# Decode attention beside a gated FFN: engine instructions in written order, and the masked weights one slot later

## The chip, the cores and the metric

The kernel runs on one core of a Trainium2 chip. The metric is the device time in microseconds (us) of one execution. Engines: PE is the matmul engine, DVE the vector engine, ACT the scalar engine; SP only issues the loads and the final store. In the traces here every engine runs its instructions in the order in which they were compiled for it (DVE's 471, for instance, before and after), and this case is about what that order is. In the tables, "span" is the length of the profiled execution, about 1.8 us shorter than its device time.

## The reference

```python
# B=4 sequences, 1 new token, D=640; H=32 heads, Dh=192, 8192 keys, of which the last W=2048 count
xn = layernorm(x)
q = (xn @ wq) -> [4, 32, 1, 192]
scores = einsum("bhqd,bhkd->bhqk", q, k_cache[:, :, -W:]) * 192**-0.5
o = einsum("bhqk,bhkd->bhqd", softmax(scores), v_cache[:, :, -W:])
attn = o.reshape(4, 1, 32 * 192) @ wo
ffn = (silu(xn @ w1) * (xn @ w3)) @ w2        # F = 1536
return x + attn + ffn                          # all bf16
```

The work is dominated by bytes: 32 heads, each with a K tile and a V tile of 3 MiB.

## The kernel before

A head's K lies in SBUF as 128 rows (32 key groups of 4 sequences) of 64 keys. A head is worked in four quarters `u` of 16 keys. DVE multiplies K by q (`mult`), PE adds up each key's six groups of 32 products with an identity matrix (`adder`, 6 matmuls), DVE reduces the 32 sums that are left (`reduce_quarter`). Then comes the maximum over all keys (`chain_*`), the exponential on ACT, the masked weights `z` (DVE), and 32 value matmuls (`pv`, 8 per quarter). At the end of each pair of heads there is the pair's end (`ge_*`): totals `tb`, reciprocals `rtb`, transposes `gp` of the value sums `o_raw`, normalised `oT`, and the projection with the pair's part of `wo`.

```python
kpool = ... bufs=KBUFS   # 2 K tiles        vpool = ... bufs=VBUFS   # 3 V tiles
wopool = ctx.enter_context(tc.tile_pool(name="wo", bufs=2))
...                                          # all loads are issued on nc.sync, one queue
def mult(u):                                 # DVE
    pr = ppool.tile([P, JQ, Dh], BF16, tag="pr")
    mi = nc.vector.tensor_tensor(out=pr[:], in0=kts[h][...], in1=qbc[...], op=ALU.mult)
def adder(u):                                # PE: 6 identity matmuls 128x512
def reduce_quarter(u):                       # DVE; asked to stay behind mult(u + 2)
    ri = nc.vector.tensor_reduce(out=scs[h][...], in_=pss.pop(u)[:], axis=AX.X, op=ALU.add)
    tc.add_manual_dep(ri.ins, mult_insts[ahead].ins.name, ORDER_DEP, ...)
def chain_bc(h):                             # PE, ACT, DVE
    ...
    nc.scalar.activation(out=ex[:], in_=scs.pop(h)[:], func=ACTF.Exp, ...)
    nc.vector.tensor_tensor(out=z[:], in0=ex[...], in1=mask_b[...], op=ALU.mult)
def pv(u):                                   # PE: 8 value matmuls 8x384
...
for h in range(H):                           # the slots; u0, ul = first, last quarter of h
    if h >= KBUFS:
        add((h - KBUFS + 1) * GQ, 0, load_k, h)
    add((h - VBUFS) * GQ + GQ + L, 0, load_v, h, ...)          # L = 10
    for u in range(u0, ul + 1):
        add(u, 1, mult, u); add(u + 1, 2, adder, u)            # slot, phase within it
        add(u + 2, 4, reduce_quarter, u); add(u + L, 3, pv, u)
    add(ul + 2, 5, chain_lmax, h); add(ul + 3, 4, chain_tr, h)
    add(ul + 4, 5, chain_gmax, h); add(ul + 5, 4, chain_bc, h)
for hg in range(NG):                         # a pair of heads
    a = (hg + 1) * HG * GQ - 1 + L
    add(a - GQ - L if hg < NG - 1 else a - L + 3, 0, wo_load, hg)
    add(a - 2, 6, ge_sum, hg); add(a - 1, 6, ge_tot, hg); add(a, 6, ge_norm, hg)
    add(a + 1, 3, ge_tr, hg); add(a + 2, 2, ge_copy, hg); add(a + 3, 3, ge_proj, hg)
... # FFN pieces (cut)
for s in sorted(sched): ...                  # the functions are called slot by slot, phase by phase
```

Before, a scheduler reorders what is written. The compiled order on PE and DVE is therefore not the slots' order. Listed from the compiled programs, with `x` counts of matmuls, a pair of heads runs like this:

```
PE : sums x12, max transpose, sums x12, max broadcast, values x32,
     sums x12, max transpose, sums x12, max broadcast, values x24, tb, values x8, gp, projection
DVE: ... gmax, gneg, z, mult, reduce, mult, reduce, mult, lmax, reduce, mult, reduce,
     gmax, gneg, z, rsm, rtb, oT, mult, reduce, ...
```

## Time and profile before

The time before was 594.14 us, the median of 3 executions (593.74 to 596.72).

| before | us |
|---|---|
| span of the profiled execution | 595.0 |
| first multiply / first multiply of the last head | 31.6 / 558.3 |
| a pair of heads in the second half | 34.14 |
| what DMA would need for a pair: 13.07 MB at 427 GB/s | 30.6 |
| drain: from the last head's first multiply to the end | 36.7 |

The pair is an average over the heads 15 to 31: the time between their first multiplies, divided by 8.

The page of the kernel before: first the busy time of each engine, then, in 40 equal slices, the granted TensorE clock in tenths, the busy share of the DMA engines in tenths, and what they moved.

```profile
PE 493.5 (83%) x2339; PEld 239.4 (40%) x2339; DVE 345.6 (58%) x471; ACT 50.4 (8%) x151; POOL 1.1 (0%) x8
...
PEclk9898979799797979989797988979798997979798
DMA  8999999999999998989799898979899798979900
GB/s 362 430 429 425 421 435 422 438 387 427 427 427 392 407 439 333 431 322 428 320 430 396 359 431 329 429 316 431 348 403 431 324 427 334 427 321 417 357 1 0
```

The slices two to eight lie between 421 and 438 GB/s. From the sixteenth slice (about 223 us) on, most second slices fall to 316 to 333: DMA is made to wait. The Trainium skill, "HBM Reference", Specifications (TRN2), gives about 425 GB/s for a core that streams alone, and the trace agrees. No engine is full. The waits view of the kernel before says who stood still and for what (engine, line, what it was about to make, whom it waited for: us in all, times, longest):

```profile
DVE oT L292 <- PE gp L282: 65.2, 16, 8.2
DVE z L240 <- ACT ex L237: 65.1, 31, 3.4
DVE rtb L274 <- PE tb L269: 59.9, 15, 4.4
PE o_ps L251 <- DVE z L240: 36.7, 30, 2.5
PE ps L196 <- DVE sc L204: 29.4, 49, 1.2
...
DVE pr L184 <- DMA kt<-in_A_k_cache_dram: 0.6, 1, 0.6
```

The multiplies hardly ever wait for K.

K is freed by the fourth multiply of a head. The load queue's own waits (SPq; line 91 loads K) and its timeline show it:

```profile
SPq L91 <- DVE pr L184: 426.5, 29, 21.1
```

```profile
409.16 0.53 SPq L91 DMA_DIRECT2D kt<-in_A_k_cache_dram  x1
430.55 0.54 SPq L91 DMA_DIRECT2D kt<-in_A_k_cache_dram  x1
443.30 0.53 SPq L91 DMA_DIRECT2D kt<-in_A_k_cache_dram  x1
```

The queue stands 426.5 us for multiplies, and K loads are issued alternately 21.4 and 12.75 us apart. In 21.4 us DMA could move 9.1 MB at 427 GB/s (an estimate), but the K and V issued at its start are 6.3 MB.

### The profile page before, as it was taken

What the parts mean: (1) busy time and instruction counts of PE and PEld (TensorE: products, weight loads), DVE (VectorE), ACT (ScalarE), POOL (GpSimd) and SP (SyncE); (2) the same over time, 40 slices, a digit from 0 to 9 for tenths busy, and PEclk for the clock granted to TensorE, in tenths of its full rate; (3) what the DMA queues carried; (4) which work ended last, traced back from release to release, by engine and by line L of the source; (5) the groups of instructions that cost most, each with busy time, mean ns of one, the idle gap of its engine ahead of it and who ended that gap; (6) DMA issues with size and microseconds to landing.
All of it is one profiled execution on the core that took longest, in us unless ns stands there. A gap on an engine that the chain in (4) does not pass through costs nothing.

```text
span 595.0 us, 5593 instructions
## 1 busy us (share of the span) xinstructions
PE 493.5 (83%) x2339; PEld 239.4 (40%) x2339; DVE 345.6 (58%) x471; ACT 50.4 (8%) x151; POOL 1.1 (0%) x8
## 2 busy tenths in 40 slices
PE   2857878889988888888888888878888888888887
PEld 1323434444544344434344343434444343433444
DVE  2197376676437748284765838285664828467531
ACT  2101100003210100001000000000010000001010
POOL 0000000000000000000000000000000000000000
PEclk9898979799797979989797988979798997979798
DMA  8999999999999998989799898979899798979900
GB/s 362 430 429 425 421 435 422 438 387 427 427 427 392 407 439 333 431 322 428 320 430 396 359 431 329 429 316 431 348 403 431 324 427 334 427 321 417 357 1 0
DMA packets 13000, 223.31 MB, mean 375 GB/s; under 512 B 1448, under 2 KB 1456, under 8 KB 4144
## 3 DMA queue, kind: packets, MB, share of 16 engines
q1 hardware_dynamic: 12976, 222.97, 89.0%
q8 instruction: 18, 0.29, 0.2%
q14 instruction: 6, 0.05, 0.0%
HBM read 222.96 MB, written 0.01 MB: 375 GB/s over the span
## 4 chain that ended last, share of the span: by engine, by line
PE 55%; DVE 36%; ACT 5%; DMA 3%; issue 1%; SPq 0%; ACTq 0%
PE o_ps L251 30%; DVE pr L184 22%; PE ps L196 12%; DVE sc L204 10%; PE gp L282 6%; DMA wt<-in_A_wq_dram 3%; ACT ex L237 2%; DVE z L240 2%; PE qps L168 2%; PE mt L230 2%; ACT o_raw L259 1%; PE gt L319 1%; DVE oT L292 1%; ACT negm L233 1%; PE tb L269 1%
## 5 line engine op out<-in xcount | busy, mean ns | idle before, releaser
L196 PE MATMUL ps<-pr,idb 128*128 128x512 bf16 x768 | 210.3, 426 | 32.3 <-DVE sc L204 29.4
L184 DVE TENSOR_TENSOR pr<-kt,qbc 128x3072 bf16<-128x3072 bf16 x128 | 223.9, 1750 | 1.0 <-DMA kt<-in_A_k_cache_dram 0.6
L251 PE MATMUL o_ps<-vt,z 128*8 128x384 bf16 x1024 | 178.1, 331 | 37.0 <-DVE z L240 36.7
L196 PEld LDWEIGHTS <-idb 128*128 128x128 bf16 x768 | 80.5, 107 | 154.2 <-issue 91.7
L251 PEld LDWEIGHTS <-z 128*8 128x8 bf16 x1024 | 86.2, 88 | 113.1 <-DVE z L240 39.3
L204 DVE TENSOR_REDUCE sc<-ps 128x16 f32<-128x512 f32 x128 | 87.7, 685 | 15.5 <-PE ps L196 15.3
L240 DVE TENSOR_TENSOR z<-ex,mask_b 128x256 bf16<-128x256 bf16 x32 | 13.6, 425 | 65.1 <-ACT ex L237 65.1
L292 DVE TENSOR_TENSOR oT<-gp,rtb 64x12 bf16<-64x12 f32 x32 | 5.4, 168 | 65.4 <-PE gp L282 65.2
L282 PE MATMUL gp<-idf,o_raw 8*128 8x4 f32 x192 | 36.1, 313 | 8.4 <-ACT o_raw L259 8.4
L282 PEld LDWEIGHTS gp<-idf,o_raw 8*128 8x128 f32 x192 | 34.7, 257 | 14.4 <-ACT o_raw L259 14.3
L274 DVE RECIPROCAL rtb<-tb 128x8 f32<-128x8 f32 x16 | 3.3, 208 | 60.1 <-PE tb L269 59.9
L259 ACT COPY o_raw<-o_ps 8x384 f32<-8x384 f32 x32 | 15.0, 468 | 191.5 <-PE o_ps L251 191.5
L233 ACT COPY negm<-mt 128x1 f32<-128x1 f32 x32 | 5.1, 159 | 306.9 <-PE mt L230 306.9
L301 PE MATMUL acc_231<-wo_t,oT 128*4 128x512 bf16 x48 | 25.6, 601 | 6.6 <-DVE oT L292 6.2
L168 PE MATMUL qps<-wt,xnT 128*128 128x512 bf16 x60 | 17.2, 456 | 5.6 <-DMA wt<-in_A_wq_dram 5.6
L174 DVE CAST qbc<-qps 128x512 bf16<-128x512 f32 x6 | 3.8, 685 | 19.5 <-PE qps L168 19.5
L302 PE MATMUL acc_232<-wo_t,oT 128*4 128x128 bf16 x48 | 14.8, 309 | 0.0
L230 PEld LDWEIGHTS mt<-ones_ff,gneg 1*128 1x128 f32 x64 | 9.4, 182 | 13.5 <-issue 13.5
L168 PEld LDWEIGHTS <-xnT 128*128 128x128 bf16 x60 | 6.8, 113 | 15.6 <-issue 10.5
L230 PE MATMUL mt<-ones_ff,gneg 1*128 1x1 f32 x64 | 12.1, 256 | 0.0
L301 PEld LDWEIGHTS <-oT 128*4 128x4 bf16 x48 | 5.3, 110 | 16.9 <-issue 8.3
L237 ACT ACTIVATE ex<-sc,negm 128x64 bf16<-128x64 f32 x32 | 11.1, 348 | 1.0
(60 smaller groups left out, 104.8 us busy)
## 6 DMA issues: line engine op xcount, KB each, us to landing
kt<-in_A_k_cache_dram SPq DMA_DIRECT2D x32, 3072.0 KB, 13.5
vt<-in_A_v_cache_dram SPq DMA_DIRECT2D x31, 3072.0 KB, 20.9
wo_t<-in_A_wo_dram SPq DMA_DIRECT2D x16, 480.0 KB, 18.7
wt<-in_A_wq_dram SPq DMA_DIRECT2D x2, 3072.0 KB, 13.3
vt<-in_A_v_cache_dram SPq DMA_DIRECT2D x4, 768.0 KB, 14.0
w_718<-in_B_w_dram SPq DMA_DIRECT2D x1, 1920.0 KB, 15.2
w_930<-in_B_w_dram SPq DMA_DIRECT2D x1, 1920.0 KB, 16.8
wt<-in_A_wq_dram SPq DMA_DIRECT2D x1, 1536.0 KB
```

The lines of the kernel that those rows point to most:

```text
L168: nc.tensor.matmul(qp[:], lhsT=xnT[:, kc].rearrange("p a b -> p (a b)"), rhs=wq_rows[kc][:, (c0 + i) * QC:(c0 + i + 1) * QC], start=(kc == ...
L184: mi = nc.vector.tensor_tensor(out=pr[:], in0=kts[h][:, g * JQ:(g + 1) * JQ, :], in1=qbc[:, h * Dh:(h + 1) * Dh].unsqueeze(1).to_broadcast ...
L196: nc.tensor.matmul(ps[:], lhsT=idb[:], rhs=pr[:, :, kk * DD:(kk + 1) * DD], start=(kk == 0), stop=(kk == NK - 1))
L204: ri = nc.vector.tensor_reduce(out=scs[h][:, g * JQ:(g + 1) * JQ], in_=pss.pop(u)[:], axis=AX.X, op=ALU.add)
L230: nc.tensor.matmul(mt[:, P:P + 1], lhsT=gneg[:].rearrange("o p b -> o (p b)"), rhs=ones_ff[0:1, 0:1], start=True, stop=True)
L237: nc.scalar.activation(out=ex[:], in_=scs.pop(h)[:], func=ACTF.Exp, bias=negm[:, 0:1], scale=SCALE, accum_out=rsums[hg][:, hl:hl + 1])
L240: nc.vector.tensor_tensor(out=z[:], in0=ex[:].unsqueeze(2).to_broadcast([P, NJ, B]), in1=mask_b[:].unsqueeze(1).to_broadcast([P, NJ, B]), ...
L251: nc.tensor.matmul(o_ps[:], lhsT=z[:, j:j + 2, :], rhs=vt[:, j:j + 2, :], start=(j == 0), stop=(j == NJ - 2))
L259: nc.scalar.copy(out=o_raws[hg][:, :, hl, :], in_=o_pss.pop(h)[:].rearrange("r (two d) -> r two d", two=2))
L282: nc.tensor.matmul(gp[:, i, :], lhsT=orf[:, part * QW + i:(part + 1) * QW:RPP], rhs=idf[0:2 * B, part * B:(part + 1) * B], start=(part == ...
L301: nc.tensor.matmul(acc0[:], lhsT=oT[:, i, :], rhs=wo_t[:, i * D:i * D + N0], start=st, stop=sp)
L302: nc.tensor.matmul(acc1[:], lhsT=oT[:, i, :], rhs=wo_t[:, i * D + N0:(i + 1) * D], start=st, stop=sp)
```

## The change

Its intent: no scheduler, so that every engine takes its instructions in the order in which the slots are written. `z` gets a function and a slot of its own, one slot after the exponential, so that DVE need not stand behind ACT.

```diff
+    ctx.enter_context(tc.manual_schedule())
 ... (mult_insts, ORDER_DEP and the add_manual_dep in reduce_quarter are removed)
     def chain_bc(h):
         ...
         nc.scalar.activation(out=ex[:], in_=scs.pop(h)[:], func=ACTF.Exp, ...)
+        exs[h] = ex
+
+    def chain_z(h):
+        ex = exs.pop(h)
         z = small.tile([P, NJ, B], BF16, tag="z")
         nc.vector.tensor_tensor(out=z[:], in0=ex[...], in1=mask_b[...], op=ALU.mult)
 ...
         add(ul + 5, 4, chain_bc, h)
+        add(ul + 6, 5, chain_z, h)
```

Afterwards, PE alternates 6 sums and 8 values of a head that is nine quarters older. On DVE, two multiplies with their reductions lie between gneg and z. The pieces of the pair's end lie one slot apart from each other. The order of the loads does not change.

More of the change, by code (lines that the diff above doesn't have):

```diff
@@ L83 @@
     v_win = A_v_cache[:, :, Sk - W:Sk, :]
-    kts, vts, prs, pss, scs, zs = {}, {}, {}, {}, {}, {}
+    kts, vts, prs, pss, scs, exs, zs = {}, {}, {}, {}, {}, {}, {}
     wos, o_pss, o_raws, rsums, chs, ges = {}, {}, {}, {}, {}, {}
-    mult_insts = {}
-    ORDER_DEP = mybir.DependencyInfo(mybir.DependencyClass.NoSync, mybir.DependencyReason.SCHED_ONLY)
     def load_k(h):
@@ L183, in mult @@
         pr = ppool.tile([P, JQ, Dh], BF16, tag="pr")
-        mi = nc.vector.tensor_tensor(out=pr[:], in0=kts[h][:, g * JQ:(g + 1) * JQ, :],
-                                     in1=qbc[:, h * Dh:(h + 1) * Dh].unsqueeze(1).to_broadcast([P, JQ, Dh]),
-                                     op=ALU.mult)
+        nc.vector.tensor_tensor(out=pr[:], in0=kts[h][:, g * JQ:(g + 1) * JQ, :],
+                                in1=qbc[:, h * Dh:(h + 1) * Dh].unsqueeze(1).to_broadcast([P, JQ, Dh]),
+                                op=ALU.mult)
         prs[u] = pr
-        mult_insts[u] = mi
         if g == GQ - 1:
@@ L203, in reduce_quarter @@
             scs[h] = small.tile([P, NJ], FP32, tag="sc", name="sc")
-        ri = nc.vector.tensor_reduce(out=scs[h][:, g * JQ:(g + 1) * JQ], in_=pss.pop(u)[:], axis=AX.X, op=ALU.add)
-        ahead = min(u + 2, NU - 1)
-        if ahead in mult_insts and ahead > u:
-            tc.add_manual_dep(ri.ins, mult_insts[ahead].ins.name, ORDER_DEP, reason="vector engine issue order")
+        nc.vector.tensor_reduce(out=scs[h][:, g * JQ:(g + 1) * JQ], in_=pss.pop(u)[:], axis=AX.X, op=ALU.add)
     def chain_lmax(h):
```

## The prediction

> **What bounds the kernel now.** A serial hand-over between PE and DVE, not one engine. In the steady state (timeline, 400 to 434 us) two heads take 34.15 us. Their traffic, two K tiles, two V tiles and one output-weight tile, is 13.07 MB. Where the DMA share is 1.00 (windows 60:100 and 140:180) the core moves 427 GB/s, which makes 30.6 us. The Trainium skill, "HBM Reference", Specifications, gives about 425 GB/s for a core streaming alone; the trace agrees. From 220 us on, the DMA share falls to 0.84 to 0.94: K loads are issued 21.4 and 12.75 us apart, because a K buffer frees only when the head's fourth multiply is done. PE is idle 101.5 of 595 us; the waits view gives 36.7 us for the masked weights z (about 1.2 per head), 29.4 for score reductions, 8.4 for o_raw, 6.2 for oT. DVE is busy only 58%. Multiplies hardly wait for K (0.6 us in all): DMA follows compute.
>
> **What the change does.** No arithmetic, bytes or buffers change. Before, the scheduler puts all 32 value matmuls of a head in one block straight after z, and two quarters of score sums together; at each pair's end value block, transposes, oT and next multiply run in series. After, PE alternates 6 score sums with 8 value matmuls of work nine quarters older, and z, gmax, oT each stand a slot or more ahead of their users. So the exposed latencies should go.
>
> **Cost per pair after.** PE: eight slots of 1.46 us (6 sums) + 1.46 us (8 value matmuls) = 23.4; transposes 2.25; projection 1.6 to 2.8; max chains and totals about 2: some 29.5 us at full clock, less where groups overlap. DVE: eight times 2.27 plus about 3 = 21. Both are under DMA's 30.6 us. So I expect the bound to become DMA: K landing.
>
> The clock: after each transpose phase PE ran sums every 0.43 instead of 0.22 us for about 5 us. The Trainium skill, "TensorE: Matmul & The Clock Gate", Part 1, gives half clock after an idle window of about 3.4 us; the trace fits (0.56 wait, 2.25 of tiny matmuls, 0.44 wait). With other matmuls around them these cold stretches should become rarer, granted clock from 0.905 to about 0.95; but PE now waits for K in gaps, which may keep some.
>
> **Sum.** Bytes: 223.3 MB at 427 GB/s = 523, plus 2.5 of start: last load lands near 525 (before: near 565). The last K lands some 20 us earlier; from there I count about 47 us: four slots 12, remaining value work, transposes and projections 25, final FFN matmuls (now behind the last projection) 4 to 5, output 5. The tail after the last load stays about 28 us (before 29.5). 525 + 28 = 553; a little for imperfect queueing: 555 us. Range 543 to 573. Faster by over 2%: 0.93, within: 0.06, slower: 0.01.
>
> **What would show it.** DMA share 0.97 or more and about 425 GB/s up to 520 us; multiplies waiting for K tens of us; PE's waits for z and sc near zero; PE busy still near 480 to 500; value groups of 8.
>
> **What would make it wrong.** PE cold more often, so that a pair costs PE 32 us or more (then about 575); output-weight loads, which wait in the one load queue for a projection, holding up the next K; value buffers freeing later and stalling V loads; a longer drain, since ten quarters of value work are left at the end.

## More of the kernel before

The timeline of the kernel before, around the end of a pair (start, duration, instruction; in brackets the idle time of its engine before it, and who ended it):

```profile
412.25 0.42 DVE L240 TENSOR_TENSOR z<-ex,mask_b 128x256 bf16<-128x256 bf16 x1 [2.08 <-ACT ex L237]
412.59 0.16 DVE L263 TENSOR_TENSOR rsm<-rsum,mask_f 128x8 f32<-128x8 f32 x1
...
417.15 0.21 DVE L274 RECIPROCAL rtb<-tb 128x8 f32<-128x8 f32 x1 [4.40 <-PE tb L269]
...
419.06 2.25 PE L282 MATMUL gp<-idf,o_raw 8*128 8x4 f32 x12 [0.56 <-ACT o_raw L259]
421.35 0.35 DVE L292 TENSOR_TENSOR oT<-gp,rtb 64x12 bf16<-64x12 f32 x2 [4.00 <-PE gp L282]
421.73 1.76 DVE L184 TENSOR_TENSOR pr<-kt,qbc 128x3072 bf16<-128x3072 bf16 x1
```

DVE's next multiply (421.73) depends on none of the lines above it; its K landed at 406.6. It only stands behind z, rtb and oT in DVE's order. Per pair DVE stops 2.08 us twice at z, 4.40 at rtb and 4.00 at oT, 12.56 us in all.

## The result, and the profile after

Measured: 566.87 us median of 4 executions (564.86 to 568.88). The ratio to before is 0.9533, 95% interval 0.9488 to 0.9579. All ratios here are the mean time of one kernel's fast runs over the mean of the other's fast runs of the same rounds, so they are not quite the ratio of the medians quoted. Executions over 1.5% slower than the fastest of the same kernel are left out of the means.

| us | before | predicted | after |
|---|---|---|---|
| time | 594 | 555 (543 to 573) | 566.9 |
| last head's first multiply starts | 558.3 | about 505 | 515.3 |
| drain from there | 36.7 | about 47 | 47.8 |
| last load has landed | 565.6 | near 525 | 540.7 |
| a pair of heads in the second half | 34.14 | 30.6 | 31.64 |
| mean granted clock | 0.905 | 0.95 | 0.924 |

Before, the last head's K had landed 14.1 us ahead of its first multiply; after, the multiply starts as K lands, so the prediction's time for this K stands in that row. 43 us were gained before the last head, and 11.1 us were given back in the drain: when the last multiply is done, value work of eleven quarters is still ahead, before the change of eight. The page after, the same lines:

```profile
PE 489.6 (87%) x2339; PEld 221.8 (39%) x2339; DVE 343.1 (61%) x471; ACT 50.4 (9%) x151; POOL 1.1 (0%) x8
...
PEclk9898879988889999899979898988989898988998
DMA  8999999999999999999999999999999999999630
GB/s 360 423 435 427 427 425 435 425 428 424 430 432 425 424 428 421 404 429 418 415 438 374 432 396 429 399 413 417 387 431 396 436 406 423 419 426 404 247 154 0
```

The deep dips are gone, shallow ones (374 to 418) remain from the middle on. The waits view after, lines that answer to those of before:

```profile
DVE pr L183 <- DMA kt<-in_A_k_cache_dram: 116.6, 30, 7.0
...
PE ps L194 <- DVE sc L202: 51.6, 22, 5.4
DVE oT L291 <- PE gp L281: 40.8, 16, 4.6
DVE z L239 <- ACT ex L232: 13.2, 7, 3.8
DVE rtb L273 <- PE tb L268: 5.2, 1, 5.2
```

DVE's stops at oT, z and rtb have shrunk from 190 to 59 us, and the multiplies now wait for K: compute follows DMA. PE's 51.6 us before its sums is for the most part the same wait passed on (no multiply, no sums): 16 of the 22 waits, 46.6 us, end 2.4 us after a wait of DVE for K ends.

Why are there still dips? The waits of the load queue itself, kernel after:

```profile
SPq L99 <- PE o_ps L250: 238.2, 29, 15.6
SPq L105 <- PE mt L225: 159.4, 13, 12.9
SPq L90 <- DVE pr L183: 51.2, 17, 9.7
```

L99 loads V, L105 the pair's part of wo, L90 K. The queue waits 159.4 us for a wo buffer (the profile names the PE matmul just behind the projection that frees it). The timeline of the load queue shows what stands behind that:

```profile
381.45 0.53 SPq L99 DMA_DIRECT2D vt<-in_A_v_cache_dram  x1
394.56 0.33 SPq L105 DMA_DIRECT2D wo_t<-in_A_wo_dram  x1
394.98 0.54 SPq L90 DMA_DIRECT2D kt<-in_A_k_cache_dram  x1
```

The K load of 394.98 goes into the buffer whose last multiply began at 381.89 and took 1.75 us. It could have started at 383.7, some 11 us earlier, but the wo load was ahead of it. DMA ran dry, as the stretch view shows (its last two columns are the DMA share and GB/s). Here are 392 to 396 us of the kernel after, and then the same of experiment e1 below, in which the wo load never waits:

```profile
392.00:396.00 4.00, 4.00 (x24) 1.86 (x22) 2.25 (x4) 0.60 (x3) 0.00 (x0) 1.00 0.60 224
```

```profile
392.00:396.00 4.00, 4.00 (x23) 1.81 (x23) 2.24 (x5) 0.00 (x0) 0.00 (x0) 1.00 0.99 422
```

### The profile page after: what moved, and what is told of

Its sections match the earlier page's. It is cut to its first block, busy times and chain, and to the rows that moved or that the text cites. A ratio compares the mean times of both kernels' runs of the same rounds, so it can differ in the third digit from the quotient of the medians.

```text
span 563.1 us, 5565 instructions
## 1 busy us (share of the span) xinstructions
PE 489.6 (87%) x2339; PEld 221.8 (39%) x2339; DVE 343.1 (61%) x471; ACT 50.4 (9%) x151; POOL 1.1 (0%) x8
## 4 chain that ended last, share of the span: by engine, by line
DMA 49%; PE 34%; DVE 15%; ACT 1%; issue 0%; SPq 0%; ACTq 0%
DMA kt<-in_A_k_cache_dram 46%; PE o_ps L250 13%; DVE pr L183 11%; PE ps L194 11%; PE gp L281 4%; DMA wt<-in_A_wq_dram 3%; DVE sc L202 3%; PE qps L167 2%; PE acc_233 L300 1%; PE f_3727 L393 1%; PE gt L318 1%; PE mt L225 1%; DVE z L239 0%; PE mt L211 0%; ACT ex L232 0%
## 5 line engine op out<-in xcount | busy, mean ns | idle before, releaser
L183 DVE TENSOR_TENSOR pr<-kt,qbc 128x3072 bf16<-128x3072 bf16 x128 | 223.2, 1745 | 116.6 <-DMA kt<-in_A_k_cache_dram 116.6
L194 PE MATMUL ps<-pr,idb 128*128 128x512 bf16 x768 | 203.2, 404 | 54.6 <-DVE sc L202 51.6
L250 PE MATMUL o_ps<-vt,z 128*8 128x384 bf16 x1024 | 205.4, 349 | 1.1 <-ACT o_raw L258 1.1
L250 PEld LDWEIGHTS <-z 128*8 128x8 bf16 x1024 | 82.9, 90 | 129.2 <-issue 76.1
L194 PEld LDWEIGHTS <-idb 128*128 128x128 bf16 x768 | 72.5, 102 | 149.5 <-issue 89.4
L291 DVE TENSOR_TENSOR oT<-gp,rtb 64x12 bf16<-64x12 f32 x32 | 5.4, 168 | 41.0 <-PE gp L281 40.8
L239 DVE TENSOR_TENSOR z<-ex,mask_b 128x256 bf16<-128x256 bf16 x32 | 13.4, 419 | 13.9 <-ACT ex L232 13.2
L300 PE MATMUL acc_233<-wo_t,oT 128*4 128x512 bf16 x48 | 14.8, 379 | 0.4 <-DVE oT L291 0.4
L232 ACT ACTIVATE ex<-sc,negm 128x64 bf16<-128x64 f32 x32 | 11.1, 348 | 1.0
L301 PE MATMUL acc_234<-wo_t,oT 128*4 128x128 bf16 x48 | 10.5, 219 | 0.0
L216 DVE TENSOR_REDUCE gmax<-mt 1x4 f32<-1x128 f32 x32 | 8.7, 273 | 2.2 <-PE mt L211 1.8
L211 PE MATMUL mt<-idf,lmax 128*1 128x128 f32 x32 | 8.6, 270 | 0.0
## 6 DMA issues: line engine op xcount, KB each, us to landing
wt<-in_A_wq_dram SPq DMA_DIRECT2D x2, 3072.0 KB, 13.2
```

The source lines that it names most:

```text
L183: nc.vector.tensor_tensor(out=pr[:], in0=kts[h][:, g * JQ:(g + 1) * JQ, :], in1=qbc[:, h * Dh:(h + 1) * Dh].unsqueeze(1).to_broadcast([P, ...
L194: nc.tensor.matmul(ps[:], lhsT=idb[:], rhs=pr[:, :, kk * DD:(kk + 1) * DD], start=(kk == 0), stop=(kk == NK - 1))
L239: nc.vector.tensor_tensor(out=z[:], in0=ex[:].unsqueeze(2).to_broadcast([P, NJ, B]), in1=mask_b[:].unsqueeze(1).to_broadcast([P, NJ, B]), ...
L250: nc.tensor.matmul(o_ps[:], lhsT=z[:, j:j + 2, :], rhs=vt[:, j:j + 2, :], start=(j == 0), stop=(j == NJ - 2))
L300: nc.tensor.matmul(acc0[:], lhsT=oT[:, i, :], rhs=wo_t[:, i * D:i * D + N0], start=st, stop=sp)
L301: nc.tensor.matmul(acc1[:], lhsT=oT[:, i, :], rhs=wo_t[:, i * D + N0:(i + 1) * D], start=st, stop=sp)
```

## The experiments

Two questions were to be settled, one for each half of the story: where the missing 12 us went (A: wo ahead of K in the queue; B: PE, clock included; C: V buffers freed late), and what had made the gain (D: DVE's stops; rivals: alternation on PE, the shift of z, the written order as such).

### e1: three wo buffers

```diff
-    wopool = ctx.enter_context(tc.tile_pool(name="wo", bufs=2))
+    wopool = ctx.enter_context(tc.tile_pool(name="wo", bufs=3))
```

> One edit to the changed kernel: three output-weight buffers instead of two. Theory A (the missing 12 us against the prediction are DMA gaps: the output-weight load waits in the one load queue until a projection frees its buffer, and the next K load, whose own buffer is free some 11 us earlier, stands behind it): the wait of the output-weight load falls from 159 us to near 0, the last head's K lands near 505 us instead of 515, time 553 to 559. Theory B (PE is the limit, half clock included, and the loads only follow it): 565 to 569, unchanged. Theory C (value tiles free too late): 563 to 568, the wait only moves to V loads.

Measured: 554.5 us (552.7 to 555.6), ratio 0.9323 [0.9272, 0.9375]. The last head's K was there at 506.1 us, a pair took 30.68 us, and the queue's wait for wo is gone. What the 280 us from 220 to 500 look like in the kernel before, then after, then e1:

```profile
220.00:500.00 280.00, 238.59 (x1125) 115.92 (x1124) 174.17 (x233) 17.09 (x64) 0.00 (x0) 0.90 0.90 380
```

```profile
220.00:500.00 280.00, 256.15 (x1235) 116.21 (x1233) 182.79 (x249) 19.19 (x72) 0.00 (x0) 0.93 0.99 414
```

```profile
220.00:500.00 280.00, 257.31 (x1251) 117.06 (x1249) 191.00 (x259) 19.68 (x73) 0.00 (x0) 0.93 1.01 428
```

380, 414 and 428 GB/s. PE's busy time and clock are the same in the second and third line, so PE was not what held the kernel back in the middle. A is confirmed, B and C are rejected for the middle of the run. The busy share of DMA alone (0.99 against 1.01) would hardly have shown it; the GB/s do.

### e2: the wo load two slots later, behind K

```diff
-        add(a - GQ - L if hg < NG - 1 else a - L + 3, 0, wo_load, hg)
+        add(a - GQ - L + 2 if hg < NG - 1 else a - L + 3, 0, wo_load, hg)
```

> One edit to the changed kernel: the output-weight load is issued two slots later, behind the K load that it stood before; still two buffers. Theory A says that the order in the queue is the fault, not the buffer count: the same 553 to 560 as with three buffers. B and C: 565 to 569.

Measured: 554.13 us (553.1 to 554.3), ratio 0.9316 [0.9268, 0.9365]; K of the last head at 506.4. No buffer was added, and the time is that of e1. The queue still waits 116.6 us for wo, but the next K is no longer behind it. The order in the queue was the fault.

### e3: z in its old slot, written order kept

```diff
-        add(ul + 6, 5, chain_z, h)
+        add(ul + 5, 5, chain_z, h)
```

> Half of the change undone: written order kept, z again in the slot of its exponential. DVE then stands about 1.8 us per head before z (exp chain) and starts the next multiply late; I estimate up to 0.8 us per head on PE, partly hidden behind DMA: 568 to 580. Rival (the z shift is cosmetic, the written order does it all): 565 to 569.

Measured: 568.9 us (566.7 to 572.6), ratio 0.9589 [0.9522, 0.9656]; the changed kernel's was 0.9533 [0.9488, 0.9579]. The intervals overlap: no effect of the shift of z is shown, and the measured time lies in both expected ranges. DVE's stop at z rises from 13.2 to 41.4 us, its wait for K falls from 116.6 to 93.8: the stop is paid out of time in which DVE would have waited for K anyway. The converse, the kernel before with its scheduler and z one slot later, was built and not run: its order on PE, DVE, ACT and SP comes out identical to before, because the scheduler puts z straight behind the exponential whatever the slot.

### e4: the value matmuls in one block again

```diff
-            add(u + L, 3, pv, u)
+            add(u0 + L, 3, pv, u)
```

> The changed kernel, but the 32 value matmuls of a head in one block, as in the kernel before, at the slot where its first quarter stood. If alternating quarters of sums and values on PE is what gains: above 575. If what gains is that z, gmax and oT are ready before their users (they still are here): 560 to 570, and V buffers free three slots earlier.

Measured: 561.9 us, the median of three fast runs (559.7 to 566.3), ratio 0.9463 [0.9386, 0.9539]; a fourth run, 570.0, was slow and is left out. No gain from the alternation of 6 sums and 8 values, the most visible thing in the new order, is shown. The expectation was wrong in one respect: with the block, oT and gmax are not ready before their users. DVE's stops there rise from 40.8 and 1.8 us to

```profile
DVE oT L291 <- PE gp L281: 81.4, 16, 7.4
DVE gmax L216 <- PE mt L211: 36.0, 16, 4.6
```

and its wait for K falls from 116.6 to 52.7: these stops, too, are hidden.

### e5: every consumer right behind its producer

```diff
-            add(u + L, 3, pv, u)
+            add(ul + 4, 8, pv, u)
-        add(ul + 5, 4, chain_bc, h)
-        add(ul + 6, 5, chain_z, h)
+        add(ul + 4, 6, chain_bc, h)
+        add(ul + 4, 7, chain_z, h)
 ... (ge_sum, ge_tot, ge_norm, ge_tr, ge_copy, ge_proj)
+            add((hg + 1) * HG * GQ - 1 + 4, 9, fn, hg)      # all six in one slot
```

> The written order of the changed kernel, but each consumer written right behind its producer, so that DVE's order becomes nearly that of the kernel before: maximum, z, value block, totals, oT in one slot, two output-weight buffers. Theory D (before, DVE's in-order stream sets the pace: 21.6 us of work per pair plus about 12 us in which it stands at z, rtb and oT while its next multiplies are ready; the gain of the change is distance, not the written order as such): 583 to 605, DVE idle before z, rtb and oT together above 140 us, nearly no wait for K. Rival (the scheduler's order of sums and reductions, or the alternation on PE, is what cost before): 560 to 575.

Measured: 651.27 us (646.3 to 654.7), ratio 1.0978 [1.0905, 1.1051]. The direction is that of D, but the range was missed by 46 us: I had one quarter of sums less ahead of the value block than the kernel before, so that DVE's reductions also waited behind the block (67.7 us) and the reciprocals longer (113.0). Written order can be worse than the scheduler's.

### e6 and e7: only one half tight, with three wo buffers

```diff
 e6: ge_tot, ge_norm, ge_tr, ge_copy, ge_proj, which were in slots a - 1 to a + 3:
+            add(a, 7, fn, hg)
 e7: as e5 for pv, chain_bc and chain_z; the pair's end as in the changed kernel
```

> Three output-weight buffers, and only the pair's end written tight (totals, transposes, oT, projection in one slot). DVE then waits some 6 us per pair at oT; 21.6 + 6 + about 1 stays under the 30.6 us of DMA, so theory D says that it hides: 553 to 562. If any stop of DVE costs its full length: 575 or more.

> Three output-weight buffers, and only z and the value block written tight behind the maximum; the pair's end loose. DVE waits about 4 to 5 us per pair at z, PE 2.4 more: D says under or just at DMA's pace, 553 to 566. If the stops cost their full length: 575 or more.

Measured: e6 558.76 us (556.4 to 559.6), ratio 0.9413 [0.9374, 0.9451]; inside its range: the stops at the pair's end hide. e7 578.21 us (578.1 to 578.8), ratio 0.9755 [0.9727, 0.9782]: above its range, and inside that of its rival (575 or more: stops cost their full length). But it inherits e5's fault: DVE's reductions wait 128.0 us behind the value block, so e7 says nothing about z alone; e10 does.

### e8: three wo buffers and the value block

The edits of e1 and e4 together.

> Three output-weight buffers and the value block of e4 (all loose). If loads already run back to back with three buffers, the block adds nothing in the middle; it takes about 0.4 us of PE per head off the drain: 549 to 555. If V buffers freeing late still cost DMA time: 545 or less.

Measured: 556.22 us (555.8 to 558.0), ratio 0.9387 [0.9358, 0.9417]. That is 1 us above the range, and no better than e1. V buffers that free three slots earlier brought nothing here. DVE's stops at oT and gmax are as in e4 (84.9 and 35.8 us). Four V buffers, the direct test of C, do not fit: the build reports too little SBUF even with one product buffer less.

### e9: the sequence of the kernel before, in written order

```diff
-            add(u + 1, 2, adder, u)
-            add(u + L, 3, pv, u)
-        add(ul + 2, 5, chain_lmax, h)
-        add(ul + 3, 4, chain_tr, h)
-        add(ul + 5, 4, chain_bc, h)
-        add(ul + 6, 5, chain_z, h)
+            add(u, 4.5, adder, u)
+            add(ul + 4, 8 if u < ul else 8.6, pv, u)
+        add(ul + 3, 1.5, chain_lmax, h)
+        add(ul + 3, 4.4, chain_tr, h)
+        add(ul + 4, 6, chain_bc, h)
+        add(ul + 4, 7, chain_z, h)
 ... ge_sum and ge_tot (phase 8.5), ge_norm to ge_proj (phase 9) in slot (hg + 1) * HG * GQ + 3
```

> The changed kernel's written order, with the slots set so that steady-state PE and DVE sequences are those of the kernel before (two quarters of sums, maximum, value block of 32, pair's end at once; e5 had one quarter of sums less ahead of the block, and missed its range). If the written order as such is worth nothing and only the sequence counts: 588 to 600, a pair in about 34 us, DVE idle before z, rtb and oT about 12 us per pair, as before. If the scheduler's other doings cost time: 570 or less.

Measured: 610.84 us (609.9 to 612.3), ratio 1.0293 [1.0247, 1.0338]. The total missed its range, yet the part it was made for is met to the hundredth: a pair takes 34.15 us, as before (34.14), and the stops in a steady pair are again 2.08 (2.09) at z, 4.40 and 4.00. The longer total is not from the steady part: the last head starts 10.0 us later than before, most of it already there at the K loads behind the FFN pieces (200.52 against 191.53 us), and the drain is 3.7 us longer. There the written order was not a copy of the scheduler's. So in the steady part the written order as such is worth nothing: the sequence on the engines makes the pace. The waits of e9:

```profile
DVE rtb L273 <- PE tb L268: 72.0, 16, 6.1
DVE z L239 <- ACT ex L232: 70.4, 32, 4.5
DVE oT L291 <- PE gp L281: 63.9, 16, 4.0
```

### e10: as e9, but the pair's end spread over slots as in the changed kernel, three wo buffers

```diff
 (against e9)
+    ge_sum a - 2, ge_tot a - 1, ge_norm a, ge_tr a + 1, ge_copy a + 2, ge_proj a + 3   (as in the changed kernel)
+    wopool bufs=3
```

> As e9, but the pair's end (totals, transposes, oT, projection) spread over later slots as in the changed kernel, and three output-weight buffers so that these loads do not hold up K. Theory D: of DVE's 12 us of stops per pair the 8.4 at rtb and oT go, some 4 at z stay: 21.6 + 4 to 6 is below DMA's 30.6, so most of the gain: 556 to 572. If the stop at z is what sets the pace: 580 or more.

Measured: 552.52 us (552.3 to 552.8), ratio 0.9309 [0.9263, 0.9356]. Below the range, and better than the changed kernel, although z and the value block stand as tight as before and DVE stops at z more than before. It differs from e9 in two things, but in e9 the queue waits only 0.6 us for a wo buffer, so the third buffer is not what e9 lacked; the loose pair's end is:

```profile
DVE z L239 <- ACT ex L232: 77.1, 32, 4.4
DVE pr L183 <- DMA kt<-in_A_k_cache_dram: 60.5, 27, 5.4
DVE rtb L273 <- PE tb L268: 20.0, 6, 8.4
```

### The stops as a sum

Adding, for each kernel, DVE's stops at z, rtb, oT, the reductions and gmax (waits view, whole run, divided by 16 pairs) to the 21 us of DVE's own work in a pair (34.14 less 12.56 of stops and 0.5 before a reduction) gives an estimate of the pace that DVE can keep. DMA needs 30.6. The row "before" agrees by construction, and wherever DVE hardly waits for K the sum must come near the pair, whatever made the stops; the test is in the rows where stops were taken away.

| | DVE stops, us per pair | 21 + stops | pair measured, second half |
|---|---|---|---|
| e5 | 16.1 | 37 | 37.59 |
| e9 | 13.9 | 35 | 34.15 |
| before | 12.9 | 34 | 34.14 |
| e7 | 11.7 | 33 | 32.24 |
| e8 | 8.2 | 29 | 30.94 |
| e4 | 8.1 | 29 | 30.80 |
| e10 | 6.9 | 28 | 30.79 |
| e6 | 6.1 | 27 | 31.00 |
| after | 4.2 | 25 | 31.64 (wo ahead of K) |
| e12 | 5.4 | 26 | 30.68 |
| e1 | 3.3 | 24 | 30.68 |

The measured pair is about the larger of the third column and 30.6. From 8 us of stops downward nothing more is gained, because DMA needs the time anyway. That is theory D, and also why no single stop is "the" culprit: the kernel before exceeded the allowance of some 9.5 us by about 3, and taking away either part of its stops is enough. e10 shows it for the pair's end, with z as tight as before. For z, e6 is a weak test, since its stops at rtb and oT (56.0 us) are less than half of those before (125.1); e8 is a better one, with 127.8 us at oT, rtb and gmax and only 2.0 at z.

### e11: transposes of o_raw in bf16, three wo buffers

```diff
-    o_raws[hg] = small.tile([2 * B, 2, HG, Dh], FP32, ...)        ... rhs=idf[0:2 * B, ...]
+    o_raws[hg] = small.tile([2 * B, 2, HG, Dh], BF16, ...)        ... rhs=idb[0:2 * B, ...]
```

> Three output-weight buffers, and the transposes of o_raw in bf16: PE spends about 1.1 us less per pair in the 12 tiny matmuls, and the stretch of tiny matmuls that precedes half clock is shorter. If DMA sets the pace until the last K (theory A), only the drain gains: 551 to 555. If PE still limits (theory B): 548 or less.

Measured: 547.14 us (546.8 to 547.4), ratio 0.9217 [0.9178, 0.9255], correct. Below the range of theory A (551 to 555) and inside that of B (548 or less), so the time alone would speak for B. The traces do not: K of the last head was there at 506.5 us, exactly as in e1 (506.1), so theory A stands for the middle, and the whole gain over e1 lies in the drain, which took 38.9 instead of 47.0 us. I had sized the saving wrongly: in the timelines the transposes take 0.31 instead of 2.25 us, twice in the drain and once just before it, and what stands behind the last of them ran at half clock in e1 (the projection and the first four of the twelve FFN matmuls of 512 columns, 0.63 us each) and at full clock in e11 (0.38). PE's work does set the drain.

### e12: e10 and e11 together

> The two best of the earlier runs together: the sequence of e10 (value block early, pair's end loose, three output-weight buffers) and the bf16 transposes of e11. If DMA sets the pace until the last K, that K lands near 507 us again, and the drain gets the shorter of both savings: e10 drained 43.4 us after it, less about 2 us for each of the two transposes in the drain and 1 for a warmer clock: 541 to 547. If the savings are the same microseconds (both only take PE backlog away): 547 to 550.

Measured: 545.17 us (544.3 to 546.1), ratio 0.9186 [0.9137, 0.9235], the fastest kernel, correct. K of the last head at 506.4, drain 36.1. Against e1's 554.5, e10 saved 2.0 us, e11 7.4 and e12 9.3: the two savings add up, as the first of the two expectations had it (though e1 ran in other rounds, and its ratio's interval overlaps e10's). The granted clock over the run rose to 0.991, from 0.963 in e10:

```profile
220.00:500.00 280.00, 223.47 (x1216) 106.87 (x1215) 190.45 (x258) 19.68 (x73) 0.00 (x0) 1.00 1.01 428
```

PE is 34 us less busy in this stretch than in e1 and DMA moves the same 428 GB/s. In e12 PE also still waits 39.8 us for z, more than before the change. Here a wait that was not on the pacing chain cost nothing.

## Why the prediction was right or wrong

- **The bound before: right.** Two in-order engines handing over to each other, DMA following. But the weight lay on PE's waits (36.7 us at z). e12 keeps them in full and is 49 us faster than before; what paced was DVE, whose stops delay multiplies that were ready (e9 has these stops and a pair of 34.15 us; e10, without most of those at the pair's end, 30.79).
- **What gains: partly wrong.** The prediction put the gain on distance between producer and user, which e5, e9 and e10 show, and on PE's alternation, in which e4 and e8 show no gain. The shift of z shows no effect either (e3). The total did not suffer from this, because it was summed from DMA's bytes and the drain and would be the same for any order in which DMA sets the pace.
- **The new bound, DMA: right, and the term that was mis-sized is the last head's K.** The prediction had it "some 20 us earlier" than 525, so at 505; it was there at 515.3, and that is nearly the whole distance to the measured time. The prediction allowed "a little for imperfect queueing", 2 us. The runs show 9.2 us (515.3 against 506.1 in e1) for the wo load ahead of K. The prediction had named this among what could make it wrong, with the right mechanism, and had not put it into the sum.
- **The drain: right,** 47 predicted, 47.8 measured. But it was then added to the wrong point: "the tail after the last load stays about 28 us" was 22.4 (563.1 less 540.7), because the last V loads, issued only at 523.9, and the wo and FFN loads behind them had moved the last landing to 540.7. The two errors, a landing 15.7 us later and a tail 5.6 us shorter, partly cancel, since the end hangs on the last K and not on the last landing.
- **DMA share right, rate off.** Expected 0.97 or more and about 425 GB/s; from 220 to 500 us the share was 0.99, but the rate 414 GB/s, for the same reason.
- **Waits at z and sc "near zero": half right.** z is gone from PE's list; 51.6 us before sums is mostly K's wait passed on, which the prediction should have expected where it let multiplies wait for K.
- **Clock: right in direction, too high** (0.924 for 0.95). By the clock records, a half-clock stretch follows within 1.5 us of all 16 transpose phases before, and still of 10 of 16 after.

The Trainium skill, "Perfetto Trace Analysis", Optimization Strategy (under Identifying Performance Opportunities), says to find the gaps of the engine in question and what they wait for, and that consistent bubbles can mean a buffer too few. Both fit here: the first found DVE's stops, and the second is the wo buffer of e1. e2 adds that reordering can do the same without the buffer.

What stays open: how much of e4's and e8's slightly different drains is order and how much clock was not separated; a fourth V buffer could not be tried. The length of DVE's stops depends on how fast PE gets to what DVE waits for, and the kernel before with bf16 transposes alone, which would shorten the stop at oT, was not run.

## What to carry to other kernels

When each engine takes its instructions in order, write each consumer so far behind its producer that the producer is done, and first on the engine whose next independent work frees the buffers of the loads; then compare that engine's work plus stops with what DMA needs, since stops below the difference are free. In a single load queue, a load that must wait for its buffer holds up every load behind it, so put it behind the loads whose buffers are free earlier, or give it one more buffer. A deeper software pipeline has a longer drain (here 11 us given back), and here PE set it, not DMA (in e1 the last load landed at 531.0 of 553.1 us), so small savings there counted in full.

## What the Trainium skill lacked or had wrong

- "TensorE: Matmul & The Clock Gate", Part 1, ties half clock to an idle window of about 3.4 us. Here it also followed tiny matmuls that the trace counts as busy: in the changed kernel PE was busy for all of 384 to 392 us, yet after 2.25 us of 12 fp32 matmuls of 4 columns six sums took 2.02 us (1.47 otherwise) and eight values 2.53 (1.46 otherwise), at a granted clock of 0.68 from 388 to 392. (The prediction's "the trace fits" counts such matmuls as idle, which Part 1 does not say; Part 4 has a remark of this kind, but for transpose mode alone, and these are plain matmuls.) In e1, 10 of 16 such phases were followed by half clock within 1.5 us, in e11, with bf16, none. The mean clock of e11 was no higher for that (0.927 against 0.941): its half-clock stretches came where PE had stood idle for about half or more of the 3.4 us before. Together with e10's order (0.963 alone) it was 0.991.
- No page that I found gives the cost of small fp32 matmuls with their weight loads; the skill's rule for the time of a weight load goes by columns alone. Here 12 records took 2.25 us, each with a weight load of 257 ns, against 6 in 0.31 us for the same work in bf16, each with one of 99 ns. "FP8 and Floating Point Precision", TensorE Precision Notes, speaks of four passes for true FP32; the trace shows two records per matmul (192 for 96), and does not say what one record holds.
- "DMA: Bandwidth & Descriptors", Issuing engines are not separate DMA queues, says that issuing from several engines saves only the sequencer's issue time. The page says elsewhere that the issuing sequencer does the waiting, but it does not draw the consequence that a load waiting for its buffer blocks the loads written behind it on the same issuing engine: 159.4 us of such waits, and 9.2 us before the last head (after against e1), were at stake here. Whether another issuing engine would have cured it was not tried.
- "Perfetto Trace Analysis", Identifying the Most-Contended Engine, goes by occupancy, and for DMA by HBM utilization; matmul busy time (83% here) it does not take as a measure. Before, that would have put DMA first (375 GB/s over the run); the pace was set by DVE at 58%, whose work plus in-order stops came to about 34 us per pair. The gaps that the page's next section asks for were what showed it.
